# A fixed order for all engines, idle matmuls at the start and weights cast on the way in, in a fused linear-attention and feed-forward kernel

## Chip, cores, metric

One core of a Trainium2 chip. The metric is device time in microseconds (us) per execution. Each kernel was executed several times; the profile is of one of these executions. An execution counts as *slow* when it took over 1.5% more than the fastest of the same kernel; ratios use the others, the *fast* ones. A profile also gives the *span*, from the first to the last recorded instruction. In the views, PE is TensorE (PEld its weight loads), DVE is VectorE, ACT is ScalarE, POOL is GpSimd, SP is SyncE, which issues transfers; a "q" behind a name is the part of an engine that issues. L279 is line 279 of that run's kernel. The *granted clock* is the share of TensorE's full clock, 1.0 or 0.5 in these records.

## The reference

```python
# r, k, v: (B=4, H=8, S=768, D=48); w, u: (H, D)
for t in range(S):
    cur   = outer(u * k[t], v[t])
    y[t]  = r[t] @ (state + cur)
    state = w[:, None] * state + outer(k[t], v[t])
x = y.transpose(0, 2, 1, 3).reshape(3072, 384)
h = x @ w_in                                  # 384 x 2048
g = where(h >= 1, h, where(h <= -1, 0, (h + 1) ** 2 / 4))
out = g @ w_out                               # 2048 x 384
```

## The kernel before

The sequence is cut into chunks of 128 rows. One chunk of one batch is a *unit*: 4 batches by 6 chunks make 24 units, and two units form a *block* for the feed-forward part. Within a unit, r and k are weighed by powers of w, transposed, and multiplied into a 128 by 128 score matrix per head (masked); y is scores times v plus a contribution of the state; the u term is a diagonal, added when x is formed. *Layer 1* is x @ w_in, *layer 2* is g @ w_out. A scheduler orders the instructions (`tc.block(schedule_with_timeline_sim=True)`).

```python
    man.enter_context(tc.block(schedule_with_timeline_sim=True))
    ...
    for q in range(NQ):                         # weights: float32, on the SP queue
        t = stage.tile([128, nKb, FQ], F32, name="w_in_f", tag="wf")
        nc.sync.dma_start(out=t, in_=w_in_src[:, :, q * FQ : (q + 1) * FQ])
        w_in_f.append(t)
        load()                                  # K, R, V of the next unit
    ...
    def cast_in(q):                             # and cast on DVE and ACT
        for kk in range(nKb):
            eng = nc.scalar.copy if kk == nKb - 1 else nc.vector.tensor_copy
            eng(w_in_sb[:, kk, q * FQ : (q + 1) * FQ], w_in_f[q][:, kk, :])
    ...
    def s_tr(i):                                # units 0..11 on TensorE, then by DMA
        if i >= TD:
            nc.sync.dma_start_transpose(RK, RKW[i % NR].rearrange("q h d -> q (h d)"))
            return
        tr = ps_a.tile([128, 2 * NP, 128], BF16, name="tr", tag="a")
        for p in range(NP):
            nc.tensor.transpose(tr[:, NP + p, :], pair(Kw, p), ident)
        ...
    def s_y(i):                                 # x: 8 pieces, diagonal added on DVE
        ...
        for h in range(H):
            nc.vector.scalar_tensor_tensor(
                x[:, h * D : (h + 1) * D], V[:, h, :], diag[:, h : h + 1], y[:, h, :], op0=ALU.mult, op1=ALU.add)
    ...
    prep(0); prep(1); s_tr(0); s_at(0); s_tr(1); cast_in(0); s_y(0)     # program order
    ...
    each(0, (0, 1), layer1)                     # block 0 needs x of units 0 and 1
```

## Time and profile before

| | before |
|---|---|
| time, median of 3 runs | 197.77 us (197.7 to 198.09) |
| span of the profiled execution | 199.1 us |
| busy: TensorE, DVE, ACT, GpSimd | 87, 56, 61, 56% |

The prediction below shows the busy rows, the chain and the start and end of TensorE's timeline. Two further views: First TensorE's waits over the whole run of the kernel before; the columns after the colon are us in total, times, and the longest:

```profile
PE tr L194 <- POOL RKW_171 L173: 8.8, 1, 8.8
PE xp L265 <- DVE x L238: 5.1, 5, 2.2
PE h_p L279 <- DMA xT_201<-x: 2.5, 1, 2.5
```

The array waits 8.8 us for the first weighed K, then five times for x, then once in mid-run for a transposed x. Second, the busy time of each engine in four stretches (length, then busy us of PE, weight loads, DVE, ACT, POOL with instruction counts, then granted clock, DMA share, GB/s):

```profile
25.00:60.00 35.00, 32.29 (x357) 24.86 (x354) 27.84 (x88) 31.39 (x66) 29.42 (x34) 1.00 1.00 215
60.00:100.00 40.00, 40.00 (x399) 29.14 (x399) 23.17 (x72) 24.67 (x53) 33.22 (x40) 1.00 1.16 207
100.00:140.00 40.00, 37.48 (x392) 26.91 (x391) 25.48 (x90) 23.17 (x52) 28.44 (x36) 0.96 0.85 148
```

Between 25 and 140 us, TensorE is idle for some 5 us only.

### The profile page before, as it was taken

The numbers are of one execution on the slowest core, as the hardware profiler recorded it, in microseconds if no ns is written. First come the engines' busy times: TensorE is split into PE (matmuls) and PEld (weight loads), VectorE is DVE, ScalarE is ACT, GpSimd is POOL, SyncE is SP. The second block draws the span as 40 slices with busy tenths as digits, with TensorE's granted clock in tenths as the row PEclk, the third lists the DMA queues.
The fourth block names the chain that finished last, engine by engine and source line by source line (L and its number), as shares of the span: only waits on it lengthen the run. The fifth ranks groups of instructions, "written<-read, shape, count | busy, mean of one in ns | idle before, by whom it ended". The sixth has DMA issues, their size and how long they took to land.

```text
span 199.1 us, 4592 instructions
## 1 busy us (share of the span) xinstructions
PE 172.3 (87%) x1686; PEld 125.7 (63%) x1686; DVE 111.8 (56%) x354; ACT 122.0 (61%) x251; POOL 110.8 (56%) x144
## 2 busy tenths in 40 slices
PE   0263598998989999999999959999999999999990
PEld 0141476776867677866777547677667677777750
DVE  4179979994867608842867643776576464200110
ACT  3657769999887547936558326567555356454540
POOL 7496756989976999967679386857221000000000
PEclk9999999999999999999999979999999999999999
DMA  4999989999969999999999998334315022020202
GB/s 96 201 258 264 250 195 221 243 181 268 262 131 244 173 193 169 258 195 173 253 162 216 165 168 206 76 74 132 64 35 153 2 66 66 9 79 0 82 3 89
DMA packets 100444, 30.25 MB, mean 152 GB/s; under 512 B 93504, under 2 KB 98880, under 8 KB 100416
## 3 DMA queue, kind: packets, MB, share of 16 engines
q1 hardware_dynamic: 100416, 29.90, 75.1%
q8 instruction: 15, 0.25, 0.6%
q14 instruction: 13, 0.11, 0.2%
HBM read 20.84 MB, written 4.72 MB: 128 GB/s over the span
## 4 chain that ended last, share of the span: by engine, by line
PE 66%; DMA 5%; DVE 4%; ACT 2%; POOL 1%; issue 1%; ACTq 0%; DVEq 0%
PE o_p L297 28%; PE h_p L279 26%; DVE x L238 3%; DMA xT_201<-x 3%; DMA R<-in_r_dram 2%; PE y L227 2%; PE y L224 2%; PE st L235 1%; PE xp L265 1%; PE tr L194 1%; ACT gT L285 1%; ACT RK L197 1%; POOL RKW_173 L173 0%; POOL KU L177 0%; PE tr L196 0%
## 5 line engine op out<-in xcount | busy, mean ns | idle before, releaser
L285 ACT ACTIVATE gT<-h_p 128x512 bf16<-128x512 f32 x96 | 56.8, 598 | 44.9 <-PE h_p L279 42.6
L297 PE MATMUL o_p<-w_out_sb,gT 128*128 128x384 bf16 x384 | 73.5, 327 | 0.0
L279 PEld LDWEIGHTS <-w_in_sb 128*128 128x128 bf16 x576 | 54.5, 99 | 14.5 <-issue 3.4
L297 PEld LDWEIGHTS <-gT 128*128 128x128 bf16 x384 | 36.2, 98 | 19.3 <-issue 0.7
L238 DVE SCALAR_TENSOR_TENSOR x<-V,diag,y 128x48 bf16<-128x48 bf16 x192 | 35.8, 257 | 18.5 <-PE y L227 11.1
L176 POOL TENSOR_TENSOR KU<-K,u_bc 128x384 f32<-128x384 f32 x24 | 24.5, 1021 | 1.9 <-DVE diag L213 1.6
L177 POOL TENSOR_TENSOR KU<-KU,R 128x384 f32<-128x384 f32 x24 | 24.3, 1013 | 0.3
L301 DVE COPY o_sb<-o_p 128x384 f32<-128x384 f32 x12 | 6.7, 555 | 23.8 <-PE o_p L297 23.7
L197 ACT COPY RK<-tr 128x1024 bf16<-128x1024 bf16 x12 | 12.2, 1014 | 3.9 <-PE tr L196 3.8
L182 POOL CAST V<-V 128x384 bf16<-128x384 f32 x16 | 8.1, 503 | 11.3 <-DVE x L238 7.0
L206 PEld LDWEIGHTS <-RK 48*128 48x128 bf16 x192 | 8.3, 99 | 9.5 <-issue 4.2
L213 DVE TENSOR_REDUCE diag<-KU 128x8 f32<-128x384 f32 x24 | 13.1, 546 | 2.1 <-POOL KU L177 1.9
L265 PE MATMUL xp<-ident,x 128*128 128x128 bf16 x36 | 7.9, 236 | 5.6 <-DVE x L238 5.1
L301 ACT COPY o_sb<-o_p 128x384 f32<-128x384 f32 x12 | 5.7, 476 | 7.5 <-PE o_p L297 6.4
L173 POOL TENSOR_TENSOR RKW_171<-K,Winv 128x384 bf16<-128x384 f32 x6 | 6.0, 997 | 6.9 <-ACT Winv L137 3.5
L279 PE MATMUL h_p<-xT_201,w_in_sb 128*128 128x256 bf16 x48 | 7.4, 302 | 2.5 <-DMA xT_201<-x 2.5
L173 POOL TENSOR_TENSOR RKW_177<-K,Winv 128x384 bf16<-128x384 f32 x6 | 6.2, 1029 | 6.1 <-PE st L235 3.9
L265 PEld LDWEIGHTS <-x 128*128 128x128 bf16 x36 | 3.6, 101 | 8.9 <-DVE x L238 8.0
L194 PE MATMUL tr<-ident,RKW_171 128*128 128x128 bf16 x12 | 1.4, 249 | 8.8 <-POOL RKW_171 L173 8.8
L173 POOL TENSOR_TENSOR RKW_173<-K,Winv 128x384 bf16<-128x384 f32 x6 | 6.6, 1094 | 3.6 <-DMA K<-in_k_dram 1.8
L279 PE MATMUL h_p<-xT_195,w_in_sb 128*128 128x256 bf16 x48 | 7.7, 311 | 0.1
L173 POOL TENSOR_TENSOR RKW_175<-K,Winv 128x384 bf16<-128x384 f32 x6 | 6.4, 1072 | 2.1 <-DMA K<-in_k_dram 1.6
(356 smaller groups left out, 321.9 us busy)
## 6 DMA issues: line engine op xcount, KB each, us to landing
K<-in_k_dram SPq DMA_DIRECT2D x24, 192.0 KB, 4.9
R<-in_r_dram SPq DMA_DIRECT2D x24, 192.0 KB, 4.7
V<-in_v_dram SPq DMA_DIRECT2D x24, 192.0 KB, 4.9
out_dram<-o_sb SPq DMA_DIRECT2D x24, 192.0 KB, 2.3
w_in_f<-in_moe_w_in_dram SPq DMA_DIRECT2D x4, 768.0 KB, 5.7
w_out_f<-in_moe_w_out_dram SPq DMA_DIRECT2D x4, 768.0 KB, 5.9
w_bc<-in_w_dram SPq DMA_DIRECT2D x1, 192.0 KB, 3.5
u_bc<-in_u_dram SPq DMA_DIRECT2D x1, 192.0 KB, 4.3
```

Source lines behind the costliest of these rows:

```text
L173: nc.gpsimd.tensor_mul(Kw[:, :, 0:D], K, Winv)
L176: nc.gpsimd.tensor_mul(KU, K, u3)
L177: nc.gpsimd.tensor_mul(KU, KU, R)
L197: nc.scalar.copy(RK, tr)
L206: mm(AT_p[s][:, p, :], KT[rows, p, :], RT[rows, p, :], start=True, stop=True)
L213: nc.vector.reduce_sum(diag, KU, axis=mybir.AxisListType.X)
L238: nc.vector.scalar_tensor_tensor(x[:, h * D : (h + 1) * D], V[:, h, :], diag[:, h : h + 1], y[:, h, :], op0=ALU.mult, op1=ALU.add)
L265: nc.tensor.transpose(xp[:, kk, :], x[:, kk * 128 : (kk + 1) * 128], ident)
L279: mm(h_p[:, f, :], w_in_sb[:, kk, (2 * n + f) * 128 : (2 * n + f + 1) * 128], xT[m][:, :, kk, :], start=(kk == 0), stop=(kk == nKb - 1),)
L285: nc.scalar.activation(g, h_p, AF.Square, bias=0.5, scale=0.5)
L297: mm(o_ps[m][j], gT[m][:, f, j * C : (j + 1) * C], w_out_sb[:, f, :], start=(f == 0), stop=(f == nN - 1))
L301: (nc.scalar.copy if j else nc.vector.tensor_copy)(o_sb, o_ps[m][j])
```

## The change

The intent: one fixed order for all engines, found by a search over assumed durations; layer 1 to begin as soon as one unit's x exists; weights to be cast by the transfer itself; and the array's clock to be brought up early with matmuls whose result nobody reads. The diff, cut to its core:

```diff
-    man.enter_context(tc.block(schedule_with_timeline_sim=True))
+    man.enter_context(tc.block())
+    man.enter_context(tc.manual_schedule())
+ORDER = """
+w u ld:K:0 ld:K:1 ln warm*14 ub tab:K ld:R:0 Kw:0@DVE wt uc ld:V:1 tab:R gi:0 dec ld:V:0 KU1:0 ld:R:1 Rw:0
+KU2:0 warm*41 trp:0 li:0 trc:0@DVE Vb:0 dg:0 gi:1 warm*14 at:0 st:0 mk:0:1 VD:0@POOL ld:R:2 mk:0:0 gi:2
+... (one token per operation, to the last store; @ names the engine) ..."""
+    PE_T, PE_X, PE_D, ONE, PAIR = 8, 14, 6, 2, 24   # units transposed on TensorE (r/k; x), with the
+                                                    # diagonal on TensorE; blocks with layer 1 per unit
+    RING = dict(f=36, ...)                          # 36 load buffers
+    nc.scalar.preload_act_table_set("natural_log_exp_and_others")
+    def warm(count):                                # idle matmuls, 183 in all, 139 before layer 1
+        for i in range(count):
+            mm(spare[0][:, d_out:], ident, ident, start=False, stop=False, skip_group_check=True)
+    IN = [(0, 1, "K1"), (1, 2, "R1"), (2, 3, "V1"), (3, 4, "K2")]
+    def wait_for(j, f):                             # the "hold": a copy of 1 element of a load
+        nc.gpsimd.tensor_copy(hold[0:1, j : j + 1], t[held(f)][0:1, 0, 0:1])
+    def load_in(z):
+        a, e, f = IN[z]
+        wait_for(z, f)
+        nc.gpsimd.dma_start(out=w_in_sb[:, :, a * FQ : e * FQ], in_=w_in_src[:, :, a * FQ : e * FQ])
-        nc.sync.dma_start(out=t, in_=w_in_src[:, :, q * FQ : (q + 1) * FQ])    # f32
-            eng(w_in_sb[:, kk, q * FQ : (q + 1) * FQ], w_in_f[q][:, kk, :])     # casts
+    def vdiag(i): ...    # VD = V * diagonal; then y += ident.T @ VD, and x is one copy
```

In the order, `L1:m:n:u` is group n of layer 1 of block m for unit u, `gi:z` the transfer of quarter z of w_in, `trp` and `trc` a transpose and its copy, `VD` the product of V and the diagonal. The last unit's layer 2 is also computed and stored in halves over two queues.

## The prediction

> **What bounds the kernel now.** I read the page first, then the chain that ended last in order of time, then the TensorE rows of the timeline for the stretches in which that chain is not TensorE, then the waits. From the page, the busy rows and the shares of the chain:
>
> ```profile
> PE   0263598998989999999999959999999999999990
> PEclk9999999999999999999999979999999999999999
> DMA  4999989999969999999999998334315022020202
> PE 66%; DMA 5%; DVE 4%; ACT 2%; POOL 1%; issue 1%; ACTq 0%; DVEq 0%
> ```
>
> A slice is 5 us. TensorE is the bound from about 27 us to 194 us. It does next to nothing in the first five slices, and there is one dip at slice 23 (about 115 us). The DMA row is full for the first 120 us, so transfers are the second thing to watch. DVE, ACT and POOL are each busy for some 55 to 61% of the span.
>
> The timeline of TensorE shows where the solid part starts, and at what rate:
>
> ```profile
> 25.03 2.77 PE L279 MATMUL h_p<-xT_195,w_in_sb 128*128 128x256 bf16 x12
> 28.59 1.49 PE L279 MATMUL h_p<-xT_195,w_in_sb 128*128 128x256 bf16 x12
> ...
> 113.81 0.24 PE L318 MATMUL n_p<-ones,sq 128*128 128x1 bf16 x4
> 116.52 2.52 PE L279 MATMUL h_p<-xT_201,w_in_sb 128*128 128x256 bf16 x12 [2.47 <-DMA xT_201<-x]
> ```
>
> Columns are start and duration in us. The first layer-1 work (L279) starts at 25.03 us. Its first 12 matmuls take 2.77 us, the same 12 take 1.49 us 3.6 us later: until about 27.5 us TensorE runs at half rate, though PEclk shows 9. After the 2.47 us wait at 114 to 116.5 us the half rate comes back (2.52 us). That wait is for the DMA transpose of x for block 6, behind a late GpSimd/DMA chain (102.3 to 116.5 us in the chain of waits). It is the only long one in the steady part.
>
> The end, from the timeline:
>
> ```profile
> 191.56 2.11 PE L297 MATMUL o_p<-w_out_sb,gT 128*128 128x384 bf16 x12
> 193.44 0.56 DVE L301 COPY o_sb<-o_p 128x384 f32<-128x384 f32 x1 [8.63 <-PE o_p L297]
> 193.75 0.48 ACT L301 COPY o_sb<-o_p 128x384 f32<-128x384 f32 x1 [1.40 <-PE o_p L297]
> 194.02 1.54 SPq L304 DMA_DIRECT2D out_dram<-o_sb  x2
> ```
>
> The last matmul ends at 193.7 us, the span at 199.1 us: a tail of 5.4 us.
>
> **Work of TensorE, from the chain's rates.** One layer-1 group of 6 matmuls takes 0.655 us, 8 layer-2 matmuls take 1.30 us. So layer 1 is 96 x 0.655 = 62.9 us, layer 2 is 48 x 1.30 = 62.4 us, 125.3 us together. Per attention unit: transposes 0.55 (only units 0 to 11), scores 0.37 to 0.66, y about 0.2 plus 0.19 for the state, st 0.17, x transposes about 0.2. For units 2 to 23 that is some 30 us. Thus about 156 us of work in the 168.7 us from 25.0 to 193.7: **some 12 us of loss inside, and 25 us before**.
>
> **What the Trainium skill says.** "TensorE: Matmul & The Clock Gate", Part 1: the array starts at half clock and is released after about 3.4 us of sustained activity, and a gap of that size throttles it again. The trace agrees in kind (2.77 against 1.49 us); here a wait of 2.47 us, with little work around it, sufficed. The idle matmuls aim at this. "ScalarE: Activation LUTs", Table sets: one set holds both ln and exp. The trace has two table loads of 1283 ns, the second at 5.12 us, between Ln and the first Exp; the change preloads the common set. "DMA: Bandwidth & Descriptors", SWDGE vs HWDGE: a cast inside a DMA is possible only from GpSimd; and, Issuing engines are not separate DMA queues: all issuers share the same 16 engines. So the casting DMA removes ACT and DVE work but no transfer time. No run here has shown a casting DMA yet.
>
> **The change part by part.**
>
> (1) Start. Removed before unit 0: the second table load (1.28 us), the two small wc transfers ahead of K (0.90 us of issue), the wc activations (0.4 us). Ln ends at 4.8 us; the two tables then end about 5.4 and 6.5 us (against 7.1 and 7.6), and both weighings go to DVE (0.56 us each, against 0.99 on GpSimd), so the transposes of unit 0 could start at about 7.2 us instead of 8.76. But 14 and 41 idle matmuls stand ahead of them. At 0.107 us each (the start-to-start of the early transposes and scores) the 41 alone take 4.4 us, at 0.055 us 2.3 us. I take 8 to 9.5 us, so nothing is won there. Then: transposes 0.5, copy on DVE about 0.7, scores 0.45, two masks 0.69 each, y 0.4, x as one copy of about 0.56 (instead of 8 pieces x 0.19 = 1.5 us), 3 transposes 0.2, copy 0.4; with 1.8 us for DVE work ordered in between and 1.5 us of hand-overs, about 8 us. So **the first layer 1 starts at about 16.7 us**, and, as it now needs one unit instead of two, with the array at full rate. Before: 25.03 us and then 1.3 us lost to the half rate.
>
> (2) Casts. 12 casts of w_in (8 x 0.52 DVE, 4 x 0.62 ACT) and 8 of w_out (4 x 0.62, 4 x 0.83) go: 6.6 us of DVE and 5.8 us of ACT, all before 63 us, where these engines are nearly full (9.9 us each of the 10 us from 30 to 40). On GpSimd come 8 issues and 8 tiny copies; no row tells their cost. If near 1 us each, 8 us, against about 12 of its other operations moved to DVE. Its total stays near 105 us.
>
> (3) TensorE. Layers 1 and 2 keep their work. Transposes fall from 12 to 8 units, x transposes rise from 12 to 14. The diagonal is a 384-wide matmul on 6 units (6 x 0.16 = 1 us). The norms go from 48 to 16 tiny matmuls. The order again alternates the two row halves of the scores (0.37 us for 8 in the early trace, 0.33 + 0.33 later). Left after the first layer 1: transposes 6 x 0.55 = 3.3, scores 23 x 0.4 = 9.2, y 23 x 0.2 + 20 x 0.19 = 8.4, st 18 x 0.17 = 3.1, x 13 x 0.2 = 2.6, diagonal 0.8, norms 0.5: 27.9 us. With 125.3: **153.2 us**.
>
> (4) Gaps after the first layer 1. The order puts 44 idle matmuls there, 2.4 us that the search saw as gaps. Weights: by the first layer 1, K, R, V of units 0 and 1 and all four w_in quarters want 4.3 MB; at the 253 GB/s of the stretch 8.7 to 25 us that is 17 us, plus the start, about 21 us. So the last quarter gates unit 0 of block 0 for a little, and w_out (3 MB) with units 2 to 4 (1.8 MB) ends at about 40 us. I put 4 us on these and the idle matmuls, 2.3 us on the later 130 us: 6.3 us, half of today's 12.
>
> (5) Tail. The last unit is computed and stored in halves over two queues: 4.8 us for 5.4.
>
> Sum: 16.7 + 153.2 + 6.3 + 4.8 = 181.0 us of span. The time before is 1.3 us below its span (197.77 against 199.1), so **179.7 us**.
>
> **Rivals.** (a) **Transfers become the bound.** The DMA row is full to 120 us already, and every load, RK transpose and store stays (4 more RK transposes); a faster TensorE asks for the same bytes sooner. For it: that row. Against it: today the loads end near 118 us, some 10 units ahead of what TensorE uses there, and the new ring of 36 loads lets them run further ahead. If it holds, TensorE waits for RK, x or w_out, and the time is 185 to 192 us. (b) **The fixed order stalls.** All engines now follow one order made from assumed durations; an operation that takes longer (GpSimd while DVE works beside it: one weighing on DVE took 1.35 us instead of 0.56; a late cast DMA) holds up everything behind it. Then many short waits, 5 to 10 us in all, 184 to 190 us. (c) **The idle matmuls delay real ones**, if they run at half rate ahead of unit 0: 2 us, in the sum for the most part. (d) The gain at the start is given back, as attention is the bound: POOL has about 105 us in the first 140 us, 75%, so unlikely. (e) Nearly all the gaps vanish: 174 to 176 us.
>
> **Range and chances.** The start (8 us and the half rate) is the best founded gain; the inner losses are my widest term: 6 us give or take 5, the start give or take 2. That gives 174.5 to 187.5 us. To miss a gain of 2% (193.8 us) losses would have to double today's. Faster 0.95, same 0.04, slower 0.01.
>
> **What would show it.** First L1 row of layer 1 at 15 to 18.5 us, its 12 matmuls of 128 columns in about 0.7 us, not 1.4; no casts of weights on ACT and DVE; TensorE full from about 25 us; no wait over 2 us in the middle, no half rate after 17 us; last matmul at 174 to 178 us; a tail under 5 us. I would be wrong if w_in lands after 25 us because the casting DMA is slow, if GpSimd's issues cost several us each, or if waits on DMA transposes return around blocks 4 to 8.

## The result

| | before | after |
|---|---|---|
| median of 4 runs | 197.93 us (197.7 to 199.66) | 184.17 us (182.03 to 184.81) |
| span of the profiled execution | 199.1 us | 181.6 us (time of that run: 183.59) |

The ratio is 0.9223, 95% interval 0.9133 to 0.9313. Here and below, a ratio is the mean time of one kernel's fast runs over that of the other's fast runs of the same rounds, so not quite the ratio of the medians quoted. The kernel is faster by close to 8%.

The busy rows and the chain of the page of the kernel after (a slice is now 4.5 us):

```profile
PE   6996699999999999999999999999999999999970
DMA  3999999989987989987989598999973023020121
PE 85%; DMA 7%; SPq 3%; POOL 1%; issue 0%; ACT 0%
```

The first five digits of TensorE's row are now 6 to 9, where they were 0 to 6; much of that is idle matmuls. The dip in mid-run is gone. The DMA row is still near full for most of the run. All the waits of TensorE, and the middle stretches, in the views used before:

```profile
PE y L344 <- POOL VD L302: 1.5, 1, 1.5
PE h_p L402 <- DMA w_in_sb<-in_moe_w_in_dram: 1.4, 1, 1.4
PE w_p L238 <- POOL ident masks.py:199: 1.4, 1, 1.4
PE u_p L251 <- DMA u_row<-in_u_dram: 0.4, 1, 0.4
```

```profile
25.00:60.00 35.00, 35.00 (x485) 28.58 (x481) 27.56 (x57) 24.61 (x54) 25.81 (x34) 1.00 1.01 191
60.00:100.00 40.00, 40.00 (x452) 30.47 (x450) 34.13 (x110) 27.70 (x64) 36.29 (x45) 1.00 0.94 195
100.00:140.00 40.00, 40.00 (x406) 28.95 (x405) 34.14 (x96) 28.96 (x61) 25.10 (x31) 1.00 0.92 174
```

Only two waits are left once the work has begun, 1.5 and 1.4 us, both before 22 us. TensorE is then busy without a break. The start, from TensorE's timeline after (start, duration, then what):

```profile
5.79 4.55 PE L241 MATMUL w_p<-ident 128*128 128x128 bf16 x41
10.14 0.78 PE L307 MATMUL tr<-ident,RKW 128*128 128x128 bf16 x8
...
15.41 0.32 PE L344 MATMUL y<-VD,ident 128*128 128x384 bf16 x1 [1.55 <-POOL VD L302]
...
19.03 0.83 PE L402 MATMUL h_p<-xT,w_in_sb 128*128 128x128 bf16 x12
...
21.80 0.84 PE L402 MATMUL h_p<-xT,w_in_sb 128*128 128x128 bf16 x12 [1.39 <-DMA w_in_sb<-in_moe_w_in_dram]
...
28.16 1.50 PE L402 MATMUL h_p<-xT,w_in_sb 128*128 128x128 bf16 x24
```

The 41 idle matmuls take 4.55 us at half rate, 0.107 us from start to start. The clock records have full clock granted at 10.48 us, against 28.01 us before; the PEclk row of the page shows 9 from the first slice in both, so it does not show this. From 19.03 us layer 1 of unit 0 runs, but in four pieces with idle matmuls between them. It becomes solid at 28.16 us, when unit 1 is ready.

**Where the time came from.** I summed, from the traces, the columns of all matmuls begun by a given time, idle ones and those that spread u and w left out, and turned them into us at the rate of a full layer-1 group (6 matmuls of 256 columns in 0.655 us). The whole work is 154.1 us before and 153.7 us after, so equal.

| by (us) | 30 | 40 | 60 | 80 | 100 | 120 | 140 | 160 | 176 |
|---|---|---|---|---|---|---|---|---|---|
| before: us of work begun | 7.3 | 14.7 | 31.7 | 50.7 | 69.8 | 84.8 | 103.0 | 120.8 | 136.5 |
| after | 8.9 | 18.9 | 38.6 | 58.2 | 78.3 | 98.2 | 118.3 | 137.7 | 153.7 |
| lead of after | 1.6 | 4.2 | 6.9 | 7.5 | 8.5 | 13.4 | 15.3 | 16.9 | 17.2 |

By 30 us the lead is only 1.6 us. It grows by 5.3 us from 30 to 60, where the kernel before fought with casts and waits; by 4.9 us from 100 to 120, where the kernel before waited for a transposed x and then ran 3.41 us at half clock; and by 3.8 us after 120, where TensorE shows as busy in both kernels. The traces resolve most of that last part: from 120 to 176 us a score matmul takes 79 ns on average from its start to the next in the kernel before and 39 ns after, worth 2.2 us. The kernel before mostly runs one row half of a unit's scores by itself there, some 56 ns apart; the new order alternates the two halves, and two matmuls start within 4 ns. The rest is gaps of a tenth of a us or so. The lead is larger than the 13.8 us between the medians, as the profiled execution of the kernel before was a long one (see below).

### The profile page after: what moved, and what is told of

Its sections match the earlier page's. It is cut to its first block, busy times and chain, and to the rows that moved or that the text cites. A ratio compares the mean times of both kernels' runs of the same rounds, so it can differ in the third digit from the quotient of the medians.

```text
span 181.6 us, 4993 instructions
## 1 busy us (share of the span) xinstructions
PE 171.4 (94%) x1948; PEld 133.6 (74%) x1948; DVE 121.6 (67%) x332; ACT 107.7 (59%) x229; POOL 104.9 (58%) x145
## 4 chain that ended last, share of the span: by engine, by line
PE 85%; DMA 7%; SPq 3%; POOL 1%; issue 0%; ACT 0%
PE h_p L402 35%; PE o_p L433 35%; DMA R<-in_r_dram 4%; PE A L323 4%; DMA w_in_sb<-in_moe_w_in_dram 3%; PE y L338 3%; SPq L279 2%; PE y L335 2%; PE st L379 2%; PE tr L307 2%; PE w_p L241 1%; PE xp L363 1%; POOL VD L302 1%; PE y L344 0%; POOL w_in_sb L466 0%; POOL hold L461 0%
## 5 line engine op out<-in xcount | busy, mean ns | idle before, releaser
L402 PE MATMUL h_p<-xT,w_in_sb 128*128 128x256 bf16 (+1 forms) x672 | 74.6, 257 | 1.4 <-DMA w_in_sb<-in_moe_w_in_dram 1.4
L433 PE MATMUL o_p<-w_out_sb,gT 128*128 128x384 bf16 (+1 forms) x400 | 75.3, 320 | 0.0
L327 DVE TENSOR_TENSOR AT<-A,umask 128x512 bf16<-128x512 f32 x48 | 31.2, 682 | 4.0 <-PE A L323 3.9
L355 DVE SCALAR_TENSOR_TENSOR x<-Vb,dg,y 128x48 bf16<-128x48 bf16 x144 | 26.8, 258 | 7.7 <-PE y L338 7.6
L183 ACT CAST Tbd<-T 48x192 bf16<-48x192 f32 x40 | 13.8, 348 | 18.2 <-DVE T L387 11.4
L283 POOL TENSOR_TENSOR RKW<-K,Winv 128x384 bf16<-128x384 f32 x19 | 19.4, 1021 | 3.3 <-DMA K<-in_k_dram 3.2
L283 POOL TENSOR_TENSOR RKW<-R,Wpow 128x384 bf16<-128x384 f32 x15 | 15.1, 1006 | 0.3 <-DMA R<-in_r_dram 0.3
L241 PE MATMUL w_p<-ident 128*128 128x128 bf16 x183 | 15.0, 247 | 0.0
L241 PEld LDWEIGHTS <-ident 128*128 128x128 bf16 x183 | 13.4, 113 | 2.0 <-issue 1.6
L298 DVE TENSOR_REDUCE dg<-KU 128x8 f32<-128x384 f32 x24 | 13.0, 543 | 1.2 <-POOL KU L294 1.1
```

Of the source, the lines that this page charges most:

```text
L183: (eng.copy if eng is nc.scalar else eng.tensor_copy)(to, src)
L241: mm(spare[0][:, d_out:], ident, ident, start=False, stop=False, skip_group_check=True)
L283: at_engine((name + "w", i)).tensor_mul(RKW[i % RING["W"]][:, off : off + H, 0:D], t[name, i], tab)
L298: nc.vector.reduce_sum(t["dg", i], t["KU", i], axis=AX)
L327: nc.vector.tensor_mul(t["AT", i, s], t["A", i][s], umask4)
L355: nc.vector.scalar_tensor_tensor(x[:, h * D : (h + 1) * D], t["Vb", i][:, h, :], t["dg", i][:, h : h + 1], t["y", i][:, h, :], op0=ALU.mul ...
```

## The experiments

Runs of one group share a chip and the runs of the kernel before. The changed kernel itself gave 0.9223 on one chip and, in the third group, 0.9342; before itself ranged from 196.8 to 202.7 us there. These two ratios are 2.4 us apart, so differences under some 2.5 us between variants are not settled by these times. Where profiles of single executions are quoted, they show the mechanism, not the size.

Theory: the gain is of the order and of the casting transfers; the idle matmuls bring the clock up early, but what then starts layer 1 is data. Rivals: the idle matmuls are the gain, or the price; the scheduler would do as well with the same operations; starting layer 1 after one unit is the gain.

### First group: the start (before: median 198.1 us of 11)

**e1_no_idle**: all idle matmuls removed.

```diff
-... ln warm*14 ub ... KU2:0 warm*41 trp:0 ... (and every other warm*N)
+... ln ub ... KU2:0 trp:0 ...
```

> The changed kernel without any of its 183 idle matmuls; nothing else moved. Theory A (idle matmuls are worth keeping: they release the array's clock at 10.5 us instead of some 28): the array stays at half rate until the first layer-1 work has run some 3 us, so 128-column matmuls come every 0.107 us till about 24 us, the last matmul moves 1.5 to 3 us later, time about 186 us. Rival B (they mostly stand in the way: 41 of them took 4.55 us ahead of the first transposes, which could have begun at 7.8 us): first transposes at about 7.9 instead of 10.1 us, time equal or up to 2 us shorter, since weights and the diagonal product set the start anyway.

Measured: 185.02 us, median of 6 (182.09 to 185.58), ratio 0.9245, interval 0.9155 to 0.9334. TensorE's timeline of its profiled run, one of the four slow ones:

```profile
15.05 0.48 PE L341 MATMUL y<-VD,ident 128*128 128x384 bf16 x1 [3.12 <-POOL VD L299]
...
19.15 1.44 PE L399 MATMUL h_p<-xT,w_in_sb 128*128 128x128 bf16 x12 [1.90 <-DVE xT L180]
...
30.32 1.50 PE L399 MATMUL h_p<-xT,w_in_sb 128*128 128x128 bf16 x24 [1.36 <-ACT xT L180]
```

Layer 1 starts at 19.15 us, as in the kernel after (19.03), but its 12 matmuls take 1.44 us instead of 0.83: the clock is granted only at 26.6 us. In this execution that adds up: layer 1 of unit 1, with which the solid part begins, starts at 30.32 instead of 28.16 us, and the last matmul ends at 178.3 us, 2.2 us after that of the kernel after, as theory A said. But it is a slow execution, and no fast one of this variant was traced. By the times the medians differ by 0.9 us and the ratios by 0.002, with two fast runs of six. So the idle matmuls may be worth nothing or some 2 us of the gain; that is not settled.

**e2_no41**: only the 41 ahead of the first transposes removed.

```diff
-... KU2:0 warm*41 trp:0 ...
+... KU2:0 trp:0 ...
```

> Only the group of 41 idle matmuls ahead of the first transposes is taken out. Theory (the start is set by the load of R of unit 1, landing at 13.2 us, which holds the GpSimd queue and with it the diagonal product of unit 0, and then by the third weight quarter at 21.8 us): first transposes at about 7.9 us, but y of unit 0 is still complete only at about 15.4 us, and the second layer-1 group still at about 21.8 us; time within 1 us of the changed kernel, unless the array is now at half rate through the start (then up to 1.5 us longer). Rival (the 41 delay the whole chain): all of unit 0 and the first layer 1 some 2.2 us earlier, time about 2 us shorter.

Measured: 184.78 us (182.23 to 185.05), ratio 0.9265, interval 0.92 to 0.933. The timeline (again of a slow run):

```profile
6.25 0.61 PE L305 MATMUL tr<-ident,RKW 128*128 128x128 bf16 x4 [0.43 <-DVE RKW L281]
...
15.37 0.48 PE L342 MATMUL y<-VD,ident 128*128 128x384 bf16 x1 [2.70 <-POOL VD L300]
...
20.38 0.83 PE L400 MATMUL h_p<-xT,w_in_sb 128*128 128x128 bf16 x12
```

The transposes come 3.9 us earlier and y not at all (15.37 against 15.41): it waits for VD on GpSimd. Worse, the wait of 2.70 us costs the clock: the records have half clock from 14.88 to 18.30 us. The idle matmuls do delay the first real ones, but no cost of it shows: without the 41, the last matmul of this slow execution came at 177.4 us, 1.4 us later than in the kernel after, and the times do not differ measurably.

**e3_vd_first**: on GpSimd, VD of unit 0 ahead of the second held transfer.

```diff
-dg:0 gi:1 warm*14 at:0 st:0 mk:0:1 VD:0@POOL ld:R:2
+dg:0 warm*14 at:0 st:0 mk:0:1 VD:0@POOL gi:1 ld:R:2
```

> On GpSimd, the diagonal product of unit 0 goes ahead of the held second weight cast, not behind it. Theory: the 1.55 us wait of y of unit 0 vanishes (y complete at about 13.9 us), first layer 1 at about 17.5 instead of 19.0 us; but the next layer-1 group still waits for the third weight quarter at 21.8 us, so the end moves by less than 0.5 us. Rival (every us of the start counts one for one): time 1.5 us shorter.

In the kernel after, GpSimd's timeline shows why VD was late. The hold waits 3.16 us for R of unit 1, which landed at 13.24, and everything behind it on GpSimd stands:

```profile
13.29 0.18 POOL L461 COPY hold<-R 1x1 f32<-1x1 f32 x1 [3.16 <-DMA R<-in_r_dram]
13.42 0.82 POOL L466 DMA_DIRECT2D w_in_sb<-in_moe_w_in_dram  x1
...
14.25 1.10 POOL L302 TENSOR_TENSOR VD<-V,dg 128x384 bf16<-128x384 f32 x1
```

Measured: 183.66 us (182.89 to 186.53), ratio 0.9236, interval 0.9177 to 0.9295. TensorE's timeline of this variant:

```profile
13.57 0.32 PE L342 MATMUL y<-VD,ident 128*128 128x384 bf16 x1
...
18.17 0.83 PE L400 MATMUL h_p<-xT,w_in_sb 128*128 128x128 bf16 x12 [0.59 <-DVE xT L181]
...
21.37 0.84 PE L400 MATMUL h_p<-xT,w_in_sb 128*128 128x128 bf16 x12 [1.82 <-DMA w_in_sb<-in_moe_w_in_dram]
```

The wait is gone, y comes 1.8 us and layer 1 0.9 us earlier, and the next group waits for weights instead (1.82 for 1.39 us). The end moves by 0.4 us in the profiles (last matmul 175.7 for 176.1). The gain is given back at the weights.

**e4_q_order**: the second group of layer 1 takes the quarter of w_in that landed earlier.

```diff
-warm*2 L1:0:2:0 ... sm:0:2:0 ... L1:0:1:0 ... sm:0:1:0
+warm*2 L1:0:1:0 ... sm:0:1:0 ... L1:0:2:0 ... sm:0:2:0
```

> Layer 1 of unit 0 takes the weight quarters in the order of their issue (0, 1, 2, 3) instead of 0, 2, 1, 3. The second quarter landed at 18.3 us, the third at 21.8 us. Theory (the wait for the third quarter is what sets the end): second group at about 20.3 us instead of 21.8, the third waits little, last matmul and time about 1 to 1.4 us shorter. Rival (other work fills that gap, or the fourth quarter at 25.1 us sets the end): less than 0.4 us.

Measured: 182.65 us (182.3 to 183.52), ratio 0.9212, interval 0.9166 to 0.9257. The wait for w_in is gone from the list of waits; in this execution R of unit 1 landed later (13.68 us), and the wait for VD was longer, 2.16 us. After it come 3.41 us at half clock (16.91 to 20.32), so the first layer 1 came at 21.09 us, and yet the last matmul ended at 176.6, within 0.5 us of the kernel after. By its times it is the fastest variant, under the kernel after by 1.5 us in the medians and by 0.2 us in the ratios, which lies inside the scatter between groups.

Three of these traces are of fast runs and keep the order from unit 1 on: the kernel after, e3 and e4. In each, the last matmul ends 147.9 us after the start of layer 1 of unit 1 (28.16, 27.73 and 28.66 us), wherever the first layer 1 began (19.03, 18.17 and 21.09 us). In after_again below, with a wait of 1.5 us for w_out in that part, it is 150.3 us. So what counts at the start is when that solid part begins.

### Second group: the parts (before: median 199.31 us of 7)

**e5_sched**: the operations of the kernel after, without idle matmuls, ordered by the scheduler of the kernel before.

```diff
-    man.enter_context(tc.block())
-    man.enter_context(tc.manual_schedule())
+    man.enter_context(tc.block(schedule_with_timeline_sim=True))
```

> The operations of the changed kernel without idle matmuls, but ordered by the scheduler that ordered the kernel before (from the same written order as its input), not by the fixed order. To be compared with the run without idle matmuls (185.0 us). Theory A (the fixed order is what keeps TensorE without gaps after 22 us): gaps of 5 us or more come back after the start, 191 to 197 us. Rival B (the operations themselves, casts in the DMA, one-unit layer 1, more buffers, made the gain): within 2 us of 185 us.

Measured: 226.29 us (225.86 to 227.32), ratio 1.1323, interval 1.1216 to 1.143: slower than before by 13%. GpSimd's and TensorE's timelines:

```profile
3.92 3.25 POOL L462 DMA_DIRECT2D w_in_sb<-in_moe_w_in_dram  x4
7.17 3.00 POOL L467 DMA_DIRECT2D w_out_sb<-in_moe_w_out_dram  x4
...
11.34 0.18 POOL L457 COPY hold<-K 1x1 f32<-1x1 f32 x1
```

```profile
39.59 0.48 PE L340 MATMUL y<-VD,ident 128*128 128x384 bf16 x1 [12.82 <-POOL VD L298]
...
47.87 2.60 PE L398 MATMUL h_p<-xT,w_in_sb 128*128 128x128 bf16 x24
```

Nothing ties a transfer to its hold but the order, so the scheduler issued all eight at 3.92 to 10.1 us and the holds behind them. V of unit 0, issued at 4.96 us, landed at 19.92; R of unit 1, issued at 5.74, at 25.20. Layer 1 began at 47.87 us. This mixes two causes, which e11 parts.

**e6_f32_cast**: the weights again as float32 over SP, at the same places in the order, and cast on DVE and ACT just before use.

```diff
-        wait_for(z, f)
-        nc.gpsimd.dma_start(out=w_in_sb[:, :, a * FQ : e * FQ], in_=w_in_src[:, :, a * FQ : e * FQ])
+        t["wi", z] = stage.tile([128, nKb, FQ], F32, name="w_in_f", tag="wf")       # 4 stage buffers
+        nc.sync.dma_start(out=t["wi", z], in_=w_in_src[:, :, a * FQ : e * FQ])      # w_out alike
-... L1:0:0:0 ... L1:0:2:0 ... L1:0:1:0 ... L1:0:3:0 ...         # RING f=36
+... ci:0 L1:0:0:0 ... ci:2 L1:0:2:0 ... ci:1 L1:0:1:0 ... ci:3 L1:0:3:0 ...   # and co: for w_out; f=33
```

> The weights come again as float32 over the same queue as the other loads, at the places of the casting DMAs, and are cast on DVE and ACT just ahead of their first use (33 load buffers instead of 36, to make room). Theory A (the casts matter, as DVE and ACT are on the path of the first units): first layer 1 about 1.5 us later or more, each of the first eight groups late by the casts, time 186 to 190 us. Rival B (the cast in the DMA buys nothing but idle time on engines that aren't the bound): within 1 us of the changed kernel; the weights land at about the same times, as the bytes read are the same.

Measured: 193.16 us (192.11 to 193.47), ratio 0.9648, interval 0.9557 to 0.974. That is 7.4 to 9 us slower than the two medians of the kernel after (185.73 and 184.17), 6 to 8.5 us by the ratios. TensorE's waits:

```profile
PE h_p L402 <- DVE w_in_sb L471: 5.4, 4, 2.4
PE o_p L433 <- DVE w_out_sb L482: 1.5, 4, 0.6
```

The transfers are no slower: the three quarters of w_in whose landing the trace has (the first, third and fourth issued) took 6.3, 7.2 and 6.8 us as float32, and all four 6.5, 4.9, 6.0 and 8.0 us as casting transfers in the kernel after. The loss is the casts, which stand on DVE between the quarter's landing and layer 1; with them the clock falls to half from 21.53 to 28.36 and from 31.77 to 35.18 us. The first layer 1 was not late (18.78 against 19.03 us), as theory A had expected; the solid layer 1 of unit 1 starts at 36.10 instead of 28.16 us. The order was not searched again for this variant, so 6 to 9 us is what the casts cost in this order.

**e7_tr12**: transposes as before, 12 and 12 units on TensorE.

```diff
-    PE_T, PE_X, PE_D, ONE, PAIR = 8, 14, 6, 2, 24
+    PE_T, PE_X, PE_D, ONE, PAIR = 12, 12, 6, 2, 24
-tr:8 ... tr:11 ... xT:12 ... xT:13
+trp:8 trc:8 ... trp:11 trc:11
```

> The transposes split as before the change: RK on TensorE for units 0 to 11 (not 0 to 7), x on TensorE for units 0 to 11 (not 0 to 13). TensorE work rises by 4 x 0.45 and falls by 2 x 0.17 us, ACT gets 4 copies of 1.01 us and loses one or two of 0.5. Theory A (TensorE is the bound there, and the DMA transposes are hidden): 1.2 to 1.8 us slower. Rival B (the DMA queue is the tighter one at 50 to 75 us): equal or faster.

Measured: 187.72 us (185.31 to 188.29); two of its four runs are slow, and no interval was formed. The two fast ones took 185.31 and 187.25 us, against medians of 184.17 and 185.73 us of the kernel after: the expected direction, and not settled. Two new waits of layer 1 on ACT, which has four more copies of 1.01 us, came to 1.7 us.

**e9_two_units**: layer 1 of block 0 over both units at once, as before, and still per unit for block 1.

```diff
-        per_unit = m < ONE
+        per_unit = m == 1
-L1:0:n:0 ... sm:0:n:0 ... L1:0:n:1 ... sm:0:n:1
+L1:0:2n sm:0:2n L1:0:2n+1 sm:0:2n+1          # in the places of unit 1
```

> Block 0 does layer 1 over both its units at once, as before the change (block 1 stays per unit). Theory A (starting after one unit is worth the TensorE work that it puts into the gaps before 28 us, 4 groups of 0.67 us): first layer 1 at about 26 to 28 us, last matmul and time 2 to 3 us later, 186 to 187 us. Rival B (what follows is bound by weights or by unit 2 anyway): under 1 us.

Measured: 184.47 us (183.72 to 186.32), ratio 0.9214, interval 0.9129 to 0.9299. The first layer 1 is now nearly 9 us later than in the kernel after:

```profile
27.88 2.97 PE L400 MATMUL h_p<-xT,w_in_sb 128*128 128x256 bf16 x24
```

The time does not change measurably (ratio 0.9214 against 0.9223). Both kernels begin their solid part at 28 us. But the kernel after has by then done layer 1 of unit 0, 48 matmuls or 2.6 us at full rate, in the place of idle matmuls, and this execution, which had 3.41 us at half clock from 23.72 as well, ended its last matmul at 178.8 us, 2.7 us later than the kernel after; theory A had said 2 to 3. It was the longest of the four (186.32 us); the others took 183.72 to 184.73. So starting after one unit is worth at most some 2.6 of the 13.8 us, and the times do not show that it is worth anything.

### Third group: the holds, and a version of my own (before: median 199.35 us of 11)

**after_again**: the changed kernel, unchanged, as the base of this group.

> The changed kernel once more, so that the variants of this group are compared with it on one chip. 182 to 185 us, ratio to the kernel before 0.92 to 0.93. Theory: time is the span of the profile plus some 2 us.

Measured: 185.73 us (183.86 to 187.26), ratio 0.9342, interval 0.9272 to 0.9413. In its profile (span 184.4) the one wait for w_in was 2.59 instead of 1.39 us, and layer 2 waited 1.5 us for w_out once.

**e10_nohold**: the eight one-element copies removed.

```diff
-        wait_for(z, f)
-        wait_for(NQ + z, f)
```

> The fixed order, but the casting DMAs are not held: the eight small GpSimd copies that wait for a load are taken out, so each is issued when GpSimd comes to it (the first at about 4.1 instead of 6.3 us, the second at about 10 instead of 13.4 us). Theory A (the holds keep the weights from taking the DMA engines from the first units): V of units 0 and 1 and R of unit 1 land 1 to 2 us later, unit 0 is late, time 1 to 3 us longer. Rival B (the holds mostly stand in the way, as that for R of unit 1 also stopped the diagonal product for 3.2 us): no wait of y of unit 0, quarters land 2 to 3 us earlier, time up to 1 us shorter.

Measured: 184.76 us (183.04 to 186.06), ratio 0.9302, interval 0.9234 to 0.9369. The first casting transfer is issued at 4.09 instead of 6.32 us, and V of units 1 and 0 lands at 10.29 and 11.13 us instead of 8.15 and 8.87; but R of unit 1 lands at 11.75 instead of 13.24, and VD is no longer late; instead TensorE waits 2.4 us in all for weighed rows (a slow run). In the fixed order, in which the transfers keep their place on GpSimd anyway, no gain by the holds shows.

**e11_sched_held**: e5 again, but each hold copies into an element of the part of the weights that its transfer then fills, so the scheduler must keep the two in order.

```diff
-        nc.gpsimd.tensor_copy(hold[0:1, j : j + 1], t[held(f)][0:1, 0, 0:1])
+        nc.gpsimd.tensor_copy(cell, t[held(f)][0:1, 0, 0:1])
-        wait_for(z, f)
+        wait_for(w_in_sb[0:1, 0, a * FQ : a * FQ + 1], f)          # w_out alike
```

> As the run with the scheduler's order (226 us), where the scheduler had moved all eight casting DMAs ahead of the holds, to 3.9 us; here each hold writes one element of the part of the weights that its DMA then fills, so that it can't be passed. Theory A (226 us came from unheld weights taking the DMA engines in the first 25 us): first layer 1 back from 47.9 to 20 to 24 us, time 190 to 198 us; what is left above the 185 us of the fixed order without idle matmuls is the worth of the order. Rival B (the scheduler's order itself is bad for these operations): still above 205 us.

Measured: 215.69 us (215.47 to 215.76), ratio 1.0882, interval 1.083 to 1.0935. R of unit 1 now lands at 9.60 us and the quarters of w_in at 14.6 to 25.7 us, about as early as in the kernel after (12.8 to 25.1); so some 10 us of e5's loss (10.6 by the medians, 8.8 by the ratios) were the unheld transfers. The other 30 us against e1 (185.02, also without idle matmuls) are the order itself. The first layer 1 comes at 22.09 us and the second group at 24.75, but the third at 55.36. TensorE's longest waits:

```profile
PE xp L359 <- DVE x L179: 8.4, 3, 4.3
PE y L340 <- DVE VD L298: 4.4, 3, 2.4
PE u_p L247 <- DMA u_row<-in_u_dram: 3.2, 1, 3.2
PE xp L359 <- ACT x L179: 3.1, 3, 1.9
```

Apart from u at the start (3.2 us) and a cast of V on GpSimd (2.1 us), the waits of over 1.5 us in all are for DVE and ACT. That this order gives those two engines other work first is my reading; I did not trace it. Under these waits the clock stays at half from 28.72 to 45.78 and from 49.20 to 59.44 us.

**e12_unit1**: my own order up to 30 us: VD first, quarters in the order 0, 1, 2, 3, unit 1 ahead of unit 2. The edit left 70 idle matmuls after the first transposes, not the 83 of the expectation.

```diff
-dg:0 gi:1 warm*14 at:0 st:0 mk:0:1 VD:0@POOL ... L1:0:0:0 ... at:1 ... L1:0:2:0 ... trp:2 ... L1:0:1:0 ... y:1 ...
+dg:0 warm*14 at:0 st:0 mk:0:1 VD:0@POOL gi:1 ... at:1 mk:1:0 mk:1:1 dg:1 VD:1 warm*20 L1:0:0:0 sm:0:0:0 ...
+L1:0:1:0 ... trp:2 ... y:1 x:1 ... L1:0:2:0 ... L1:0:3:0 ... L1:0:0:1 ... L1:0:1:1 ...
```

> Only the order of the operations up to about 30 us is rewritten by hand: diagonal product of unit 0 ahead of the held second cast, weight quarters in the order of their issue, and all of unit 1 ahead of unit 2 on DVE, GpSimd and TensorE; 83 idle matmuls are left of the 128 after the first transposes. Theory A (the solid part of TensorE begins only where layer 1 of unit 1 can start, 28.2 us in the changed kernel, and what lies before is filled with idle matmuls): layer 1 of unit 1 starts at 25 to 26 us, time 1 to 2.5 us shorter. Rival B (from there on the weights of layer 2, the last of which landed at 38.2 us, or unit 2 set the pace): the gain comes back as waits of TensorE between 28 and 40 us, under 0.5 us is left.

Measured: 183.8 us (183.39 to 185.47), ratio 0.9282, interval 0.9225 to 0.9339; the median is 1.9 us under that of after_again, but the intervals overlap. Unit 1 is ready earlier, and the weights are not:

```profile
25.86 3.80 PE L400 MATMUL h_p<-xT,w_in_sb 128*128 128x128 bf16 x36 [2.55 <-DMA w_in_sb<-in_moe_w_in_dram]
```

The first 12 of these 36 matmuls are the last of unit 0, so layer 1 of unit 1 begins at 27.12 us, 1.2 us earlier than in after_again, after a wait of 2.55 us for the last quarter of w_in (landed at 25.82); 3.41 us at half clock follow. At 32.91 us TensorE has waited 1.0 us more for weighed rows; at the last matmul 0.8 us is left of the 1.2 (177.8 against 178.6). So in this execution the weights' arrival bounds a faster start. No version was shown to beat the changed kernel beyond its scatter; e4 and e12 are the two that may.

Not tried: a new search of the order for the variants e6, e7 and e9, and e3 and e4 together. Nor were the diagonal on TensorE, the 36 load buffers, the early table load, the moves of work between DVE, ACT and GpSimd and the stores in halves undone, so their shares of the gain are not known.

## Why the prediction was right or wrong

The direction and the size held, and the mechanism in outline: 184.2 us lies in the range of 174.5 to 187.5, 4.5 us above the point. That the span came within 0.6 us is partly luck, as two terms were off and cancelled. Term by term:

- **Sum of the span**: 181.0 us predicted, 181.6 measured. Of the 4.5 us, 0.6 lies here and 0.6 in that the profiled run (183.59) was under the median.
- **"The time before is 1.3 us below its span (197.77 against 199.1)"** is the step that failed, and makes the other 3.3 us. It compared two different executions. In the same execution the time is about 2.0 us above the span. By that offset the profiled execution of the kernel before took some 201 us (worked out, it was not timed), as some of its timed runs did (up to 202.7). So part of what I read in that profile as loss may belong to a slow execution; whether its mid-run wait and half clock do, no run shows.
- **(1) Start**: layer 1 at 19.03, not 16.7 us, and outside the 15 to 18.5 that I gave. The single terms were near: both tables end at 5.54 and 6.42 us (5.4 and 6.5 predicted), the transposes start at 10.14 (8 to 9.5). "Next to nothing in the first five slices" was too strong: the row has 2 to 6 tenths in four of them. What was missing is a chain of waits: R of unit 1 lands late, the hold stands in front of VD on GpSimd, y waits. And the last quarter of w_in landed at 25.1 us, not at about 21. In the chain that ended last:

```profile
5.80 7.43 DMA R<-in_r_dram
...
15.76 6.00 DMA w_in_sb<-in_moe_w_in_dram
```

- And the term was the wrong marker. I let the solid part begin with the first layer 1, "as it now needs one unit instead of two". e9 takes that away, and the solid part starts at 28 us in both; what the earlier layer 1 can be worth is its own 2.6 us, and the times do not show it.
- **(2) Casts**: removing them "before 63 us, where these engines are nearly full" was right, but I put no number of us on it in the sum. Undoing it costs 6 to 9 us in this order (e6), the largest single part measured after the order itself. "No transfer time" saved, drawn from the Trainium skill's "DMA: Bandwidth & Descriptors", Issuing engines are not separate DMA queues, agrees with e6's landings (6.3 to 7.2 us as float32, 4.9 to 8.0 us as casting transfers). A casting transfer takes GpSimd 0.74 to 0.95 us to issue, as estimated.
- **(3) TensorE's work**: 153.2 us after the first layer 1 was used for the sum. From 19.03 to the end of the last matmul (176.1) are 157.1 us, so 3.9 us of gaps by this sum.
- **(4) Gaps**: 6.3 us predicted, 3.9 found: 1.39 us of waiting for w_in and otherwise idle matmuls. This and the late start cancelled each other by luck: +2.3 and −2.4 us. After 28 us TensorE shows no idle time in this profile.
- **(5) Tail**: 5.5, not 4.8 us; under 5 was expected. The halves were stored over two queues, but from the end of the last matmul it takes as long as before (5.4).

The tail in the timeline after (the last store's issue on ACT's queue, right after the last copy, which ends at 176.45; the span ends 4.7 us after it is done):

```profile
176.48 0.38 ACTq L448 DMA_DIRECT2D out_dram<-o_sb  x1
```

Of the rivals: (a), transfers as the bound, did not come about after 28 us, though they bound the start; (b), a fixed order that stalls, did not come about in the kernel after, with waits of 2.9 us in all once the work had begun; it was the scheduler's order that stalled, by 30 us. (c), idle matmuls that delay real ones, is true of the first transposes, and no effect on the end shows (e2). (d), attention as the bound, did not come about: GpSimd is busy for 104.9 us, as predicted, and TensorE waits for it only at the start (1.4 us for the identity matrix, 1.5 us for VD). (e), nearly all gaps vanish, is what the inside of the kernel shows, without the 174 to 176 us, since the start took longer.

## What to carry to other kernels

Where a kernel's start waits for data, look for the time from which its bounding engine works without a break, not for its first useful instruction: in three traces here the end followed the former by 147.9 us and not the latter. Work pulled forward into a stretch that waits for data saves its own time at most. Before giving a fast path a wait in an in-order engine, look at what stands behind it; and tie such a wait to its transfer by data, if a scheduler may reorder the two. Take time and span from the same execution before one is turned into the other.

## What the Trainium skill lacked or had wrong

- "TensorE: Matmul & The Clock Gate", Part 1: it lets the clock fall after an idle window of about 3.4 us. In these runs much less sufficed. Waits of 2.16 us (e4), 2.47 (before), 2.55 (e12) and 2.70 (e2) were each followed by 3.41 us at half clock. I laid a grid of 3.41 us on the clock records, as the page calls the window free-running: in these four runs the window that ended with the fall had a matmul running for 37, 28, 25 and 35% of it. At 56% (after, the 1.55 us wait) the clock stayed. A wait of 2.59 us in after_again fell across two windows of 61 and 63%, and cost no clock. Between some 42 and 62% both happened (e7 kept it at 51%, e9 lost it at 55%). So a partly busy window can be enough to lose the clock, and the page gives no share; the busy share alone does not decide it between 42 and 62%, and what does is open.
- "DMA: Bandwidth & Descriptors", Anatomy of one DMA: its fit, 2.0 us plus the bytes at 436 GB/s, would give a quarter of the weights (786,432 bytes read) 3.8 us. Casting transfers beside loads took 4.9 to 8.7 us here, with medians of 6.2 us (w_in) and 7.4 us (w_out). And no page says what a load loses next to one: R of unit 1, issued 0.5 us before a casting transfer, landed after 7.4 us; in e11, with the first casting transfer issued 2.5 us after it, after 4.0 us.
- "ScalarE: Activation LUTs", What ACT_TABLE_LOAD costs: it adds a drain of about 1380 ns to the load's 1283. In the trace of the kernel before, the second table load starts at 5.12 us, 0.01 us after the activation ahead of it ends, and takes 1.28 us; the next activation starts at 6.42, 0.02 us later. No drain shows there.
